# Rearranging two bundles at the start and one R in the middle of a fused convolution and channel mix

## The chip, the cores and the metric

The kernel runs on one core of one Trainium2 chip. The metric is device time in microseconds, from runs of the whole program. A profile is one execution recorded by the hardware profiler; its instructions are read as PE (TensorE matmuls), PEld (TensorE's weight loads), ACT (ScalarE), DVE (VectorE), POOL (GpSimd) and SP (the queue that issues most DMAs).

## The reference

The input x has 8 batches of 4160 rows of 192 values. Two things are computed, one after the other.

- A causal convolution of 7 taps along the rows, with softmax weights that each of 8 heads (24 values wide) has for itself: `y[s] = sum over k of w[h, k] * x[s - 6 + k]`.
- A channel mix of y: with `y_prev` the row before, `xk = y_prev + mu_k * (y - y_prev)` and `xr = y_prev + mu_r * (y - y_prev)`; then `k = relu(xk @ w_k)` (192 to 1024), `v = (k * k) @ w_v` (1024 to 192), `r = sigmoid(xr @ w_r)` (192 to 192), and the output is `r * v`.

## The kernel before

**Pairs, steps, slots, bundles.** Batches go in four pairs; one of a pair lies on partitions 0 to 63 and the other on 64 to 127, a third of the 192 channels at a time. A pair's rows are cut into steps of 512 (the first pair begins and ends with one of 256). A step of 512 has 8 K slots, one of 256 has 4. A K slot (`k_mm`, line 526) makes one PSUM tile of 128 x 2 x 512: 128 of the 1024 hidden values on partitions, for both batches and 512 rows (in a step of 256, twice as many hidden values for half the rows). Four slots are a bundle, and there are 65 bundles, then two last rounds. Their order on every engine is written out by hand: each engine does its instructions in the order in which the program names them (`tc.manual_schedule`, line 937).

**What a bundle holds.** For each of its four slots: `k_mm` on PE, `k_relu` on ACT (PSUM to the SBUF tile k_sb), `k_square` on DVE. Once in it, R (`r`, 12 matmuls; `r_out`, the sigmoid on ACT that empties it) and V (`v_rows`, line 620) for 256 rows of an earlier step: 64 matmuls in two halves, of which `half` 0 ends with a marker that ACT passes only when that half is done. `v_out` (line 643) multiplies both on DVE, which empties V's PSUM tile, and sends the product off through SP. The quads list says which rows each bundle's V takes; it lags the slots.

**The mix.** `diff` (y minus y_prev), `scale` (times mu) and `add_y` (plus y_prev) run on DVE and make xk and xr a bundle or two before they are used. The tables mix_a, mix_b, mix_c and late (lines 713 to 741) say in which bundle and at which of its four places each one stands; `run(table, b)` does what a table holds for bundle b. In the same manner rq and rs hold the R's and the sigmoids of a bundle, and xt its convolution units. rq has one entry for almost every bundle. Of the bundles that bundle_rest runs, only bundle 14 has two, for the second 256 rows of step 6 and the first 256 of step 7; bundle 17 has none.

**The convolution.** x is loaded, as bf16, in groups of rows (lines 88 to 98). For groups 0 to 2 the convolution gives y turned, channels on partitions, straight out of PE. Group 3, in bundle 1, is done as two units: `conv_mm` on PE, `conv_out` on ACT, one cast for the first unit and two for the second, into the tile y with rows on partitions. PE then transposes it (`tr`, line 437: 12 transposes in a first PSUM tile, 3 in a second), and three copies bring it to yT: the first by ACT, the two others by DVE. From group 4 on, a group is four units (`conv_tiles`, 8 matmuls; `conv_tiles_out`, one or two casts on ACT), two in a bundle: group 4 in bundles 2 and 3, group 5 in 4 and 5, later groups in every second bundle. Then `y_write` sends y to DRAM with four DMAs, and `y_read` brings it back with a transposing DMA (lines 416 to 434). For group 4 the write stands at the end of bundle 3, the read in bundle 4, and the first `diff` that needs it in bundle 6.

**PSUM.** All PSUM tiles, those of K, R, V, the transposes and the units, come from one pool of four buffers:

```python
ring = ctx.enter_context(tc.tile_pool(name="ring", bufs=4, space=bass.MemoryType.PSUM))
```

A tile's buffer is free when the last instruction that names it (the relu, sigmoid, product, cast or copy) is done, and the matmul that begins the next tile in that buffer waits for it.

**Who runs the bundles.** bundle_first and bundle_second do bundles 0 and 1, bundle_third does bundle 2, and bundle_rest the others. After bundle 4 a bundle begins with the square of the last slot of the one before, mix_a, and `v_out` of the bundle before; V's second half is the last on PE.

Of the kernel before, what the change touches and what calls it, by code (L numbers as in the profile page):

```python
# [14 lines left out]
def kernel(  # L15
# [11 lines left out]
    nc = tc.nc  # L27
# [33 lines left out]
    for p in range(NPAIR):  # L61
# [5 lines left out]
        for L in sizes:  # L67
            ns = L * NF // STEP
# [8 lines left out]
    bundles, bundle_of = [], {}  # L77
    n = 0
# [86 lines left out]
    n = groups[0][2] * 2 * D  # L165
# [271 lines left out]
    def tr(g, j):  # L437

        p, base, nb, _, _ = groups[g]
        ps = ring.tile([P, 2, 2 * BANK], BF16, tag="k", name="ps_t")  # L440
        todo = range(4 * j, min(nb, 4 * j + 4))
        view = ps[:, :, 0 : 6 * BLK].rearrange("p b (c i t) -> p b c i t", c=3, i=2)
        for i0 in todo[::2]:
            for c in range(3):
                for i in range(i0, min(nb, i0 + 2)):
                    nc.tensor.transpose(
                        out=view[:, (i - 4 * j) // 2, c, i % 2, :],
                        in_=ys[g][:BLK, i, c * P : (c + 1) * P],
                        identity=ident[:BLK, :BLK],
                    )  # L450

        for i in todo[::2]:
            n = min(2, nb - i)
            c0 = YC + base + i * BLK
            (nc.vector.tensor_copy if i else nc.scalar.copy)(
                out=yTs[p][:, :, c0 : c0 + n * BLK].rearrange("p c (n t) -> p c n t", n=n),
                in_=view[:, (i - 4 * j) // 2, :, :n, :],
            )
# [67 lines left out]
    def k_mm(n, cs=range(NC)):  # L526


        s, j = slots[n]
        L = steps[s][2]  # L530
        xk = xks[s]
        if cs[0] == 0 and n not in k_ps:
            k_ps[n] = ring.tile([P, 2, BANK], FP32, tag="k", name="ps_k")
        ps = k_ps[n]
        nf = STEP // L

        for c in cs:
            for f in range(nf):
                fs = slice((j * nf + f) * P, (j * nf + f + 1) * P)
                for i in range(2):  # L540
                    r = slice(i * Q, (i + 1) * Q)
                    nc.tensor.matmul(  # L542
                        out=ps[:, i, f * L : (f + 1) * L],
                        lhsT=wk[r, c, fs],
                        rhs=xk[r, c, :L],
                        start=c == 0 and f == 0,
                        stop=c == NC - 1 and f == nf - 1,
                    )

    def k_relu(n):  # L550
        ps = k_ps.pop(n)
        k_sb = four.tile([P, 2 * STEP], BF16, tag="k_sb", name="k_sb")
        k_sbs[n] = k_sb
        nc.scalar.activation(out=k_sb, in_=ps.rearrange("p a b -> p (a b)"), func=AF.Relu)  # L554

    def k_square(n):
        s, j = slots[n]
        L = steps[s][2]
        k_sb = k_sbs.pop(n)
        if j == 0:  # L560
            k2s[s] = three.tile([P, NF, 2 * STEP], BF16, tag="k2", name="k2")
        nf = STEP // L
        i = k_sb
        o = k2s[s][:, j, :]
        if nf > 1:
            i = k_sb.rearrange("p (b f t) -> p f b t", b=2, f=nf)
            o = k2s[s][:, j * nf : (j + 1) * nf, 0 : 2 * L].rearrange("p f (b t) -> p f b t", b=2)
        nc.vector.tensor_tensor(out=o, in0=i, in1=i, op=ALU.mult)  # L568
# [51 lines left out]
    def v_rows(s, j, half, ks=(0, 1)):  # L620

        if half == 0:
            v_ps[s, j] = ring.tile([P, 2, BANK], FP32, tag="k", name="ps_v")[:, :, 0 : 2 * D]
        for k in ks:
            for f in range(NF):
                for i in range(2):
                    q = slice(i * Q, (i + 1) * Q)
                    bank = (i + half) % 2
                    t = tile_of(s, j, 2 * bank + k)
                    nc.tensor.matmul(  # L630
                        out=v_ps[s, j][:, bank, k * D : (k + 1) * D],
                        lhsT=k2s[s][q, f, t * P : (t + 1) * P],
                        rhs=wv[q, f, :],
                        start=half == 0 and k == 0 and f == 0,
                        stop=half == 1 and k == 1 and f == NF - 1,
                    )
        if half == 0:
            nc.scalar.clobber_nop([nc.scalar.lower_ap(v_ps[s, j])])
# [4 lines left out]
    def v_out(s, j):  # L643
        p, t0, L, _, _ = steps[s]
        o_sb = three.tile([P, 4, D], FP32, tag="o_sb", name="o_sb")
        nc.vector.tensor_tensor(  # L646
            out=o_sb.rearrange("p (b t) d -> p b (t d)", b=2),
            in0=v_ps.pop((s, j)),
            in1=r_sbs.pop((s, j)),
            op=ALU.mult,  # L650
        )
        for st in range(2):
            c = t0 + 2 * j * P
            nc.sync.dma_start(
                out=out[2 * p + st, c : c + 2 * P, :].rearrange("(m p) d -> p m d", p=P),
                in_=o_sb[:, 2 * st : 2 * st + 2, :],
            )
# [24 lines left out]
    early, rq, rs, xt, mix_a, mix_b, mix_c, vq, late = ({} for _ in range(9))  # L682
# [4 lines left out]
    def conv_half(unit, half):  # L687
        if unit is not None:
            conv_mm(*unit, half)
            if half == 1:  # L690
                conv_out(*unit, nc.scalar.copy)

    for g, (p, base, nb, fb, on_pe) in enumerate(groups):
# [12 lines left out]
        if g > 4:  # L706

            b = {5: 1, 6: 2, 7: 7}.get(g)
            b = first_bundle[first_step[p]] + (-15, -11, -7, -3)[(g - 6) % 4] if b is None else b
            table = {5: mix_a, 7: mix_c}.get(g, early)  # L710
# [31 lines left out]
    for s, j, vb in quads:  # L742
        b = vb - (s == LAST)
# [6 lines left out]
        else:  # L750
            vq.setdefault(vb, []).append((s, j))

    def run(table, b):
        for fn, a in table.get(b, ()):
            fn(*a)

    def warm(ps, n):
# [81 lines left out]
    def bundle_second(b, ns):  # L839

        act_, dve_ = nc.scalar.copy, nc.vector.tensor_copy
        g = 2
        k_mm(ns[0])
        k_relu(ns[0])
        k_mm(ns[1])
        tiles = [ring.tile([P, 2, BANK], FP32, tag="k", name="ps_t") for _ in range(2)]
        outs = [tiles[0][:, 0, :], tiles[1][:, 0, :], tiles[0][:, 1, :]]
        conv_t(g, 0, outs[0], range(4))
        to_yT(g, 0, outs[0], 0, 4, dve_)
        k_relu(ns[1])  # L850
        conv_t(g, 1, outs[1], range(4))
        to_yT(g, 1, outs[1], 0, 4, dve_)
        k_mm(ns[2])
        k_relu(ns[2])
        conv_t(g, 2, outs[2], range(4))
        to_yT(g, 2, outs[2], 0, 4, act_)
        k_mm(ns[3])
        k_square(ns[0])
        run(mix_a, b)
        conv_half(xt[b][0], 0)  # L860
        k_relu(ns[3])
        conv_half(xt[b][0], 1)
        k_square(ns[1])
        run(mix_b, b)
        conv_half(xt[b][1], 0)
        conv_half(xt[b][1], 1)
        run(mix_c, b)
        run(late, b)

    def bundle_rest(b, ns):  # L870

        units = xt.get(b, [])
        quad = vq[b][0]
        if b == 4:
            v_out(*vq[b - 1][0])
        for n in bundles[b - 1][2 if b == 3 else 3 :]:
            k_square(n)
        run(mix_a, b)
        if b > 4:
            v_out(*vq[b - 1][0])  # L880
        k_mm(ns[0])
        k_relu(ns[0])
        k_mm(ns[1])
        k_relu(ns[1])
        run(mix_b, b)
        k_square(ns[0])
        k_square(ns[1])
        run(mix_c, b)
        k_mm(ns[2])
        k_relu(ns[2])  # L890
        run(rq, b)
        if units:
            run(rs, b)
        v_rows(*quad, 0)
        if not units:
            run(rs, b)
        k_square(ns[2])
        k_mm(ns[3])
        k_relu(ns[3])
        for u in units:  # L900
            conv_tiles(*u)
            conv_tiles_out(*u)
        v_rows(*quad, 1)
        run(late, b)

    def bundle_third(b, ns):

        quad = vq[b][0]
        for n in bundles[b - 1][2:]:
            k_square(n)  # L910
        run(mix_a, b)
        k_mm(ns[0])
        k_relu(ns[0])
        k_square(ns[0])
        k_mm(ns[1])
        k_relu(ns[1])
        run(rq, b)
        v_rows(*quad, 0)
        run(rs, b)
        tr(3, 0)  # L920
        tr(3, 1)
        k_square(ns[1])
        run(mix_b, b)
        k_mm(ns[2])
        k_relu(ns[2])
        v_rows(*quad, 1, (0,))
        k_mm(ns[3])
        k_relu(ns[3])
        v_rows(*quad, 1, (1,))
        run(mix_c, b)  # L930
        v_out(*quad)
        for u in xt[b]:
            conv_tiles(*u)
            conv_tiles_out(*u)
        run(late, b)

    with tc.manual_schedule():
        prologue()
# [53 lines left out]
```

## Time and profile before

| | |
|---|---|
| median of 4 runs | 415.28 us (415.21 to 415.95) |
| profiled execution | 415.45 us |
| its span, first to last instruction | 413.7 us |
| busy share of the span | PE 98%, DVE 89%, ACT 86%, POOL 16% |
| granted TensorE clock | 1.0 throughout |
| bundle 2, bundle 3 (start of the first K slot to the next bundle's) | 8.20 us, 6.69 us |
| bundle 4, bundle 5, bundle 6 | 6.40, 6.37, 6.01 us |

Rows of the timeline name, in this order, the start in us from the span's start, the time in us from the first instruction's start to the last one's end, the engine, the line of the program, the operation, what it writes and reads (written tile first), the shape written and read, and the count of instructions merged in that row. In brackets stands how long the engine sat idle before it, and what ended that. An engine's instructions overlap somewhat, so a row can end after the next one starts; on PE the ends are modelled. L542 is K, L599 is R, L630 V, L446 a transpose, L302 a unit of the convolution from group 4 on, L351 one of group 3; L554 is the relu, L610 the sigmoid, L397 and L319 the casts, L455 the copies to yT; L568 is the square, L480 diff, L516 scale, L522 add_y, L646 the product; on SP, L424 is y_write, L432 y_read, L654 an output.

### The profile page before, as it was taken

What the parts mean: (1) busy time and instruction counts of PE and PEld (TensorE: products, weight loads), DVE (VectorE), ACT (ScalarE), POOL (GpSimd) and SP (SyncE); (2) the same over time, 40 slices, a digit from 0 to 9 for tenths busy, and PEclk for the clock granted to TensorE, in tenths of its full rate; (3) what the DMA queues carried; (4) which work ended last, traced back from release to release, by engine and by line L of the source; (5) the groups of instructions that cost most, each with busy time, mean ns of one, the idle gap of its engine ahead of it and who ended that gap; (6) DMA issues with size and microseconds to landing.
All of it is one profiled execution on the core that took longest, in us unless ns stands there. A gap on an engine that the chain in (4) does not pass through costs nothing.

```text
span 413.7 us, 16805 instructions
## 1 busy us (share of the span) xinstructions
PE 404.7 (98%) x7349; PEld 302.3 (73%) x7350; DVE 369.2 (89%) x672; ACT 354.4 (86%) x428; POOL 65.5 (16%) x102
## 2 busy tenths in 40 slices
PE   7999999999999999999999999999999999999996
PEld 5567767767777777777777777777777777777795
DVE  5989799999899998989899999989989898999973
ACT  6999978889888888998888899888899888787781
POOL 8760023012040200204040020303000000000000
PEclk9999999999999999999999999999999999999999
DMA  9999989969779895997769698896973926411223
GB/s 146 178 190 203 190 206 188 246 140 189 161 129 215 156 204 138 179 230 113 195 119 233 164 172 194 103 235 118 205 164 90 194 80 160 122 61 59 79 79 115
DMA packets 137657, 65.58 MB, mean 159 GB/s; under 512 B 87388, under 2 KB 137584, under 8 KB 137584
## 3 DMA queue, kind: packets, MB, share of 16 engines
q1 hardware_dynamic: 95840, 48.42, 45.1%
q0 software_dynamic: 40944, 15.53, 33.1%
q8 instruction: 57, 0.93, 0.9%
q10 hardware_dynamic: 800, 0.57, 0.4%
q14 instruction: 16, 0.13, 0.1%
HBM read 31.62 MB, written 37.09 MB: 166 GB/s over the span
## 4 chain that ended last, share of the span: by engine, by line
PE 85%; DMA 4%; ACT 3%; DVE 3%; SPq 2%; issue 1%; POOL 0%; ACTq 0%; POOLq 0%
PE ps_v L630 37%; PE ps_k L542 36%; PE ps_r L599 7%; PE ps_c L302 3%; DMA y_dram<-y 2%; ACT k_sb L554 2%; DMA xb<-in_x_dram 1%; PE ps_v L582 1%; SPq L432 1%; ACT y L319 1%; SPq L424 1%; DVE k L568 1%; DMA out_dram<-o_sb 1%; DVE xk L522 0%; DVE o_sb L646 0%
## 5 line engine op out<-in xcount | busy, mean ns | idle before, releaser
L554 ACT ACTIVATE k_sb<-ps_k 128x1024 bf16<-128x1024 f32 x260 | 253.0, 1037 | 35.7 <-PE ps_k L542 34.2
L568 DVE TENSOR_TENSOR k<-k_sb 128x1024 bf16<-128x1024 bf16 x260 | 172.5, 685 | 29.3 <-ACT k_sb L554 28.9
L542 PE MATMUL ps_k<-xk,wk 64*128 64x512 bf16 (+1 forms) x1632 | 191.0, 367 | 1.1 <-DVE xk L522 0.6
L630 PE MATMUL ps_v<-wv,k 64*128 64x192 bf16 x4032 | 188.3, 243 | 0.1
L630 PEld LDWEIGHTS <-k 64*128 64x128 bf16 x4032 | 168.0, 94 | 13.5 <-issue 4.0
L542 PEld LDWEIGHTS <-wk 64*128 64x128 bf16 x1632 | 80.5, 94 | 59.6 <-issue 1.6
L136 POOL DMA_DIRECT2D xb<-in_x_dram x62 | 45.3, 738 | 176.2 <-issue 81.6
L646 DVE TENSOR_TENSOR o_sb<-ps_v,r_sb 128x768 f32<-128x768 f32 x64 | 60.9, 952 | 2.6 <-issue 2.4
L610 ACT ACTIVATE r_sb<-ps_r 128x768 bf16<-128x768 f32 x65 | 53.2, 821 | 11.1 <-PE ps_v L630 10.4
L319 ACT CAST y<-ps_c 128x960 bf16<-128x960 f32 (+5 forms) x84 | 50.7, 685 | 0.0
L599 PEld LDWEIGHTS <-xr 64*128 64x128 bf16 x780 | 34.5, 94 | 15.9 <-issue 1.9
L599 PE MATMUL ps_r<-wr,xr 64*128 64x192 bf16 x780 | 43.0, 243 | 1.2 <-DVE o_sb L646 1.2
L516 DVE TENSOR_SCALAR xr<-d,mu 128x512 bf16<-128x512 bf16 (+1 forms) x102 | 34.7, 346 | 0.0
L480 DVE TENSOR_TENSOR d<-yT 128x1536 bf16<-128x1536 bf16 (+3 forms) x37 | 31.7, 856 | 2.3 <-ACT yT L381 1.4
L522 DVE TENSOR_TENSOR xr<-xr,yT 128x1536 bf16<-128x1536 bf16 (+1 forms) x33 | 31.0, 939 | 1.1
L516 DVE TENSOR_SCALAR xk<-d,mu 128x512 bf16<-128x512 bf16 (+1 forms) x98 | 31.5, 350 | 0.1
L522 DVE TENSOR_TENSOR xk<-xk,yT 128x1536 bf16<-128x1536 bf16 (+2 forms) x34 | 30.5, 900 | 0.1
L302 PEld LDWEIGHTS <-toe 64*64 64x64 bf16 x448 | 9.5, 106 | 11.4 <-issue 10.6
L302 PE MATMUL ps_c<-xb,toe 64*64 64x240 bf16 (+1 forms) x448 | 16.4, 264 | 0.0
L464 POOL COPY y_tail<-yT 128x195 bf16<-128x195 bf16 x4 | 3.0, 762 | 65.4 <-DMA yT<-y_dram 65.3
L111 POOL MEMSET xb<- 32x384 bf16 x3 | 1.3, 423 | 40.5 <-DVE xb L109 40.5
L371 PEld LDWEIGHTS <-xb 128*32 128x32 bf16 (+3 forms) x264 | 5.4, 120 | 2.4 <-ACT xb L230 1.0
(59 smaller groups left out, 65.5 us busy)
## 6 DMA issues: line engine op xcount, KB each, us to landing
out_dram<-o_sb SPq DMA_DIRECT2D x128, 192.0 KB
xb<-in_x_dram POOLq DMA_DIRECT2D x40, 240.0 KB, 8.5
y_dram<-y SPq DMA_DIRECT2D x44, 210.0 KB
y_dram<-y SPq DMA_DIRECT2D x12, 168.0 KB
xb<-in_x_dram POOLq DMA_DIRECT2D x10, 192.0 KB, 6.0
xb<-in_x_dram POOLq DMA_DIRECT2D x6, 216.0 KB, 7.0
xb<-in_x_dram POOLq DMA_DIRECT2D x6, 144.0 KB, 6.1
wk<-in_moe_w_k_dram POOLq DMA_DIRECT2D x4, 96.0 KB, 5.3
```

The source lines that it names most:

```text
L136: nc.gpsimd.dma_start(out=xb[q0 : q0 + rows, lo:hi, s, :], in_=bass.AP(tensor=x.tensor, offset=x.offset + (b * S + t0 + lo * step) * D, ap ...
L302: nc.tensor.matmul(out=banks[j * Q : (j + 1) * Q, i, :, :, k * G : (k + 1) * G], lhsT=toe[q, h, q], rhs=xbs[g][q, j * m : (j + 1) * m, :, ...
L319: nc.scalar.copy(out=bass.AP(tensor=y.tensor, offset=y.offset + d, ap=[y.ap[0], [m * 2 * D, 2], [2 * D, m], [Q, 2], [1, b - a]],), in_=bas ...
L516: nc.vector.tensor_scalar(out=t[:, c, :L], in0=diffs[s][:, c, :L], scalar1=mu[:, i, c : c + 1], scalar2=None, op0=ALU.mult)
L522: nc.vector.tensor_tensor(out=o, in0=o, in1=y_of(s, sl, 0), op=ALU.add)
L542: nc.tensor.matmul(out=ps[:, i, f * L : (f + 1) * L], lhsT=wk[r, c, fs], rhs=xk[r, c, :L], start=c == 0 and f == 0, stop=c == NC - 1 and f ...
L554: nc.scalar.activation(out=k_sb, in_=ps.rearrange("p a b -> p (a b)"), func=AF.Relu)
L568: nc.vector.tensor_tensor(out=o, in0=i, in1=i, op=ALU.mult)
L599: nc.tensor.matmul(out=ps[:, i, k * D : (k + 1) * D], lhsT=xr[q, c, ts], rhs=wr[q, c, :], start=c == 0, stop=c == NC - 1,)
L610: nc.scalar.activation(out=r_sbs[s, j], in_=r_ps.pop((s, j))[:, :, 0 : 2 * D], func=AF.Sigmoid)
L630: nc.tensor.matmul(out=v_ps[s, j][:, bank, k * D : (k + 1) * D], lhsT=k2s[s][q, f, t * P : (t + 1) * P], rhs=wv[q, f, :], start=half == 0 ...
L646: nc.vector.tensor_tensor(out=o_sb.rearrange("p (b t) d -> p b (t d)", b=2), in0=v_ps.pop((s, j)), in1=r_sbs.pop((s, j)), op=ALU.mult,)
```

## The change

Four edits.

1. The first of `tr`'s three copies goes to DVE too, so that DVE makes all three.
2. In bundle 1, group 3's second unit keeps its matmuls, and its two casts move to bundle 2, behind R, its sigmoid and V's first half.
3. Bundle 2 no longer holds the transposes and group 4's units 0 and 1. The sigmoid is named ahead of V's first half; mix_b, mix_c and late come together behind the second slot's square; the third slot's square is the last step, behind `v_out`. Bundle 3, which has a branch of its own at its head, does two slots first, then the transposes with their copies, the square of bundle 2's last slot, group 4's units 0 and 1, and mix_a; the rest is as in other bundles, with units 2 and 3 behind the fourth slot.
4. `run` can take a part of a table's entries. In bundle_rest a second R, where there is one, and its sigmoid go behind the fourth slot and its relu, between V's halves. Only bundle 14 has one.

```diff
@@ tr
-            (nc.vector.tensor_copy if i else nc.scalar.copy)(
+            nc.vector.tensor_copy(
@@ run
-    def run(table, b):
-        for fn, a in table.get(b, ()):
+    def run(table, b, part=slice(None)):
+        for fn, a in table.get(b, [])[part]:
             fn(*a)
@@ bundle_second
         run(mix_b, b)
-        conv_half(xt[b][1], 0)
-        conv_half(xt[b][1], 1)
+        conv_mm(*xt[b][1], 0)
+        conv_mm(*xt[b][1], 1)
         run(mix_c, b)
@@ bundle_rest
-        if b == 4:
-            v_out(*vq[b - 1][0])
-        for n in bundles[b - 1][2 if b == 3 else 3 :]:
-            k_square(n)
-        run(mix_a, b)
-        if b > 4:
-            v_out(*vq[b - 1][0])
-        k_mm(ns[0])
-        k_relu(ns[0])
-        k_mm(ns[1])
-        k_relu(ns[1])
+        if b == 3:
+            for n in range(2):
+                k_mm(ns[n])
+                k_relu(ns[n])
+            tr(3, 0)
+            tr(3, 1)
+            k_square(bundles[b - 1][3])
+            for u in xt[b - 1]:
+                conv_tiles(*u)
+                conv_tiles_out(*u)
+            run(mix_a, b)
+        else:
+            if b == 4:
+                v_out(*vq[b - 1][0])
+            k_square(bundles[b - 1][3])
+            run(mix_a, b)
+            if b > 4:
+                v_out(*vq[b - 1][0])
+            for n in range(2):
+                k_mm(ns[n])
+                k_relu(ns[n])
         run(mix_b, b)
         k_square(ns[0])
         k_square(ns[1])
         run(mix_c, b)
         k_mm(ns[2])
         k_relu(ns[2])
-        run(rq, b)
+        run(rq, b, slice(0, 1))
         if units:
             run(rs, b)
         v_rows(*quad, 0)
         if not units:
-            run(rs, b)
+            run(rs, b, slice(0, 1))
         k_square(ns[2])
         k_mm(ns[3])
         k_relu(ns[3])
+        run(rq, b, slice(1, None))
+        if not units:
+            run(rs, b, slice(1, None))
         for u in units:
@@ bundle_third
         k_mm(ns[1])
         k_relu(ns[1])
         run(rq, b)
+        run(rs, b)
         v_rows(*quad, 0)
-        run(rs, b)
-        tr(3, 0)
-        tr(3, 1)
+        conv_out(*xt[b - 1][1], nc.scalar.copy)
         k_square(ns[1])
         run(mix_b, b)
+        run(mix_c, b)
+        run(late, b)
         k_mm(ns[2])
         k_relu(ns[2])
         v_rows(*quad, 1, (0,))
         k_mm(ns[3])
         k_relu(ns[3])
         v_rows(*quad, 1, (1,))
-        run(mix_c, b)
         v_out(*quad)
-        for u in xt[b]:
-            conv_tiles(*u)
-            conv_tiles_out(*u)
-        run(late, b)
+        k_square(ns[2])
```

## The prediction

> **What bounds the kernel now.** I read the page's head first, then the PE's own timeline for the stretches in which it stands still, then ACT, DVE and SP in those stretches. Bundle b is four K slots; bundle 2 starts at 20.56 us, bundle 3 at 28.76, bundle 4 at 35.45, bundle 7 at 54.23, bundle 15 at 103.80.
>
> ```profile
> span 413.7 us, 16805 instructions
> PE 404.7 (98%) x7349; PEld 302.3 (73%) x7350; DVE 369.2 (89%) x672; ACT 354.4 (86%) x428; POOL 65.5 (16%) x102
> ```
>
> TensorE is busy for 98% of the span, so an edit pays only where it removes a PE wait, and only if no later wait takes the gain back. After the start I find three stretches with waits. The first is bundles 2 and 3:
>
> ```profile
> 20.56 1.47 PE L542 MATMUL ps_k<-xk,wk 64*128 64x512 bf16 x12
> 21.86 0.68 PE L599 MATMUL ps_r<-wr,xr 64*128 64x192 bf16 x12
> 22.61 1.56 PE L630 MATMUL ps_v<-wv,k 64*128 64x192 bf16 x32
> 24.10 0.96 PE L446 MATMUL ps_t<-ident,y 120*128 120x120 bf16 x15
> 25.16 0.82 PE L542 MATMUL ps_k<-xk,wk 64*128 64x512 bf16 x6
> 28.76 2.33 PE L542 MATMUL ps_k<-xk,wk 64*128 64x512 bf16 x18 [0.27 <-DVE xk L522]
> 35.45 0.81 PE L542 MATMUL ps_k<-xk,wk 64*128 64x512 bf16 x6
> ...
> 20.68 1.88 ACT L397 CAST y<-ps_c 120x960 bf16<-120x960 f32 x3
> 24.98 0.77 ACT L455 COPY yT<-ps_t 128x720 bf16<-128x720 bf16 x1
> 25.79 0.78 DVE L455 COPY yT<-ps_t 128x720 bf16<-128x720 bf16 x2 [1.58 <-ACT yT L455]
> ```
>
> See that V at 22.61 starts as the last cast ends (22.56), that the K slot at 25.16 starts as the sigmoid ends (24.28 + 0.83), and that DVE stands 1.58 us until ACT's copy of the transposes is done, which makes xk late for 28.76. The PSUM ring has four buffers, and these waits fit one rule: a new tile takes the buffer released longest ago in program order.
>
> The second stretch is bundles 6 and 7, the third bundle 15:
>
> ```profile
> 36.52 3.05 SPq L424 DMA_DIRECT2D y_dram<-y  x4
> 43.39 4.85 SPq L432 DMA_TRANSPOSE yT<-y_dram  x1
> 50.22 0.96 DVE L480 TENSOR_TENSOR d<-yT 128x1536 bf16<-128x1536 bf16 x1 [0.84 <-DMA yT<-y_dram]
> 54.23 2.12 PE L542 MATMUL ps_k<-xk,wk 64*128 64x512 bf16 x18
> 56.83 0.67 PE L599 MATMUL ps_r<-wr,xr 64*128 64x192 bf16 x12 [0.48 <-DVE o_sb L646]
> ...
> 99.53 1.15 PE L599 MATMUL ps_r<-wr,xr 64*128 64x192 bf16 x24
> 102.13 1.51 ACT L610 ACTIVATE r_sb<-ps_r 128x768 bf16<-128x768 f32 x2 [0.74 <-PE ps_v L630]
> 103.52 4.01 ACT L554 ACTIVATE k_sb<-ps_k 128x1024 bf16<-128x1024 f32 x4
> 104.59 0.69 DVE L568 TENSOR_TENSOR k<-k_sb 128x1024 bf16<-128x1024 bf16 x1 [1.26 <-ACT k_sb L554]
> 105.66 0.95 DVE L646 TENSOR_TENSOR o_sb<-ps_v,r_sb 128x768 f32<-128x768 f32 x1
> 106.66 0.67 PE L599 MATMUL ps_r<-wr,xr 64*128 64x192 bf16 x12 [0.71 <-DVE o_sb L646]
> ```
>
> At 50.22 DVE waits for group 4's y, which goes out at 36.52 and comes back transposed; from there DVE runs without a pause to the product at 55.82, and the R at 56.83 waits for that. In bundle 14 two sigmoids stand in a row, so the relu of slot 4 starts only at 103.52, its square at 104.59, the product behind it at 105.66, and R of bundle 15 waits for the buffer.
>
> **Part 1: bundle 14's second R.** It is the only bundle run by bundle_rest with two R's. They take 99.53 to 100.52, 0.50 each; moving one costs PE nothing (same 24 matmuls). First half of V then starts at 100.03 and ends its issue at 101.35, the last matmul some 0.2 later; the sigmoid of the first R follows (it waits behind the marker of V's first half) at about 101.65 and lets ACT go on after 0.71, at 102.36. Slot 4 issues from 101.35; a relu starts some 0.9 after its slot's first matmul (35.45 to 36.35), so it is ready at 102.25. Relu 102.36 to 103.4, square to 104.1, the two scales in between 0.38, product 104.5 to 105.45. R of bundle 15 is then free to start when its three slots are issued, at 103.80 + 1.95 = 105.75, in place of 106.66: **0.9 us**. The second sigmoid, now behind the relu (103.3 to 104.1), gives its buffer to the third slot at 105.1, and ACT is free before the first relu of bundle 15 is ready (104.7). Queued behind the second sigmoid are only those relus; cover 0.6. Next in line in bundle 15 are V (buffer of a relu ending 105.7) and the second convolution unit (sigmoid, ends 108.24, wanted near 108.6): no wait. No DMA moves here.
>
> **Part 2: bundles 2 and 3.** Removed: ACT's transpose copy (0.77). Added: one DVE copy of the same 128x720 (0.53, the longer of DVE's two). Moved: two casts of group 3's second unit behind sigmoid and V's first half; the transposes and units 0 and 1 of group 4 behind two slots of bundle 3; DVE's product and a square forward.
> - V's first half takes the buffer of slot 1 in place of the cast's. That relu starts when the first cast ends (21.52) and takes 1.05: V at 22.62, as before. Nothing gained.
> - Slot 3: buffer of slot 2 (relu ends near 23.5), behind V at 23.94. The wait of 25.16 is gone. Slots and V's second half follow: 0.65 + 0.65 + 0.65 + 0.66, so bundle 3 could start at 26.55.
> - xk for it: DVE does two squares (to 24.6), two scales and the add (0.96), without the 1.58 pause: ready at 26.1. No wait; cover 0.45.
> - Bundle 3: two slots to 27.85, transposes 0.9 to 28.75 (the second tile wants bundle 2's product, ready at 28.2). Unit 0 at 28.75; unit 1 wants the second relu, 28.34 to 29.40: a **wait of 0.4**. The third slot wants the first transpose tile, whose two DVE copies run 28.82 to 29.80: a **wait of 0.1**, at 29.85.
> - Then slot 0.65, R 0.49, V from 30.99; from V's start to bundle 4 the row of before has 31.41 to 35.45 with 0.1 of it lost, so 3.94: bundle 4 at 34.93, **0.5 us** early. Queued behind the casts on ACT is one sigmoid and one relu, with 8.3 us of bundle for 7.9 of work.
>
> The price of the DVE copy decides here. The trace has 0.53 on DVE and 0.77 on ACT for one shape. [...]
>
> **What of the 0.5 survives.** Bundle 7 hangs on group 4's y. The last cast before the write ended at 36.50; by the same steps it ends at 35.98 (relu of slot 4 from 33.16, casts behind it), 0.52 early. SP's order doesn't change: bundle 2's output (two DMAs, now some 1.4 earlier than 29.59, among the loads, with nothing waiting for them), write, bundle 3's output, read; so the outputs push nothing. On POOL's queue nothing is moved: group 6's tile and loads stay ahead of bundle 2. But the write now meets the tail of the input loads. [...] The DMA view has 238 packets of SP's queue from 34 to 35 us beside 205 of the loads, and 243 from 38 to 39 beside 45: nearly no loss, 0.5 kept. I take **0.4**, ends 0 and 0.5. PE's own 0.5 is capped by it: bundle 7's R comes 0.4 earlier, and after it no row shows PE waiting for a transfer.
>
> **Sum.** 0.9 + 0.4 = 1.3. The profiled run took 415.45 with a span of 413.7; span 412.4, run 414.15. The median of the runs is 0.17 below the profiled one: **414.0 us**, 0.3% faster. A measurement of this kernel tells some 0.2%, 0.83 us, from no change.
>
> **Rivals.**
> - Only part 1 pays, 0.18: the write meets the loads, or the copies are slow, and y lands at its old time. For it: the loads' queue holds 120% of an engine set's time from 36 to 37. 415.28 - 0.9 = 414.4, on the edge of what can be told.
> - More is gained, 0.10: y lands early enough that bundles 6 and 7 lose their waits too (0.25 and 0.65 against a seamless start), with part 2's 0.5: 415.28 - 0.9 - 0.5 - 0.9 = 413.0. Against it: the write can't start before ACT's casts.
> - Part 1 doesn't do what it says, 0.08: R of bundle 15 waits for another buffer. Only 0.4 is left: 414.9.
> - Slower, 0.14: bundle 3 now holds four convolution units' casts on ACT, 3.5 us beside 4.4 us of relus and sigmoid, in a bundle of 8.3; if the ring makes PE and ACT wait for each other there, group 4's write is late, and each us on it is a us at 50.22. It turns the sum at casts ending 0.9 later than before, at 37.4, and measurably at 38.2; at 38.9 it gives 416.8. Against it: my steps leave 0.5 the other way.
>
> **Numbers.** The forecast has 0.50, its own range 413.5 to 414.5. Faster: nearly all of it, half of the first rival and the second, 0.67; same 0.19; slower 0.14. Range 413.2 to 415.1: it leaves out the slower rival and half of the deeper gain.
>
> **What would show it.** V of bundle 2 still near 22.6; bundle 3 near 26.6, bundle 4 near 34.9; no wait of DVE on ACT at L455; y's write near 36.0, DVE's wait for yT ending near 49.8; R of bundle 7 near 56.4; in bundle 15 R straight after K, 105.75 less 0.4. Wrong would be a longer wait for unit 1 or the third slot of bundle 3, a y that lands no earlier, or a new wait of R.

## The result, and the profile after

The changed kernel takes 414.18 us (median of 31 runs), the kernel before 415.39 us over its runs beside them: a ratio of 0.9972 (95% interval 0.9966 to 0.9977), 1.2 us faster (1.0 to 1.4). The forecast was 414.0, 1.3 us under the median of before. Two later series of the same kernel gave 0.9979 (0.9971 to 0.9987) and 0.9974 (0.9963 to 0.9985).

The execution profiled with this result is not a typical one. A first input load landed late (ACT waits 1.35 us for x_f, where before it waited 0.32), bundle 2 started at 21.55 us where before it started at 20.56, and PE waited for one more load, that of wv, which took 11.6 us from issue to landing in place of 9.5. From the PE timeline of that execution (start, length in us, engine, line, operation, tiles, shapes, count; in brackets the idle time before the row and its releaser):

```profile
21.55 1.47 PE L542 MATMUL ps_k<-xk,wk 64*128 64x512 bf16 x12
22.85 0.67 PE L599 MATMUL ps_r<-wr,xr 64*128 64x192 bf16 x12
24.57 1.49 PE L630 MATMUL ps_v<-wv,k 64*128 64x192 bf16 x32 [1.04 <-DMA wv<-in_moe_w_v_dram]
```

The first V waits for its weights. That execution took 415.79 us, the slowest of the 31. I therefore read the change from a second profile of the same program, after_again (414.21 us, span 412.5). Its head and its PE timeline, for the lines shown of before:

```profile
span 412.5 us, 16801 instructions
PE 403.5 (98%) x7349; PEld 300.9 (73%) x7350; DVE 370.3 (90%) x673; ACT 353.7 (86%) x427; POOL 65.3 (16%) x102
...
20.45 1.47 PE L542 MATMUL ps_k<-xk,wk 64*128 64x512 bf16 x12
...
26.43 1.47 PE L542 MATMUL ps_k<-xk,wk 64*128 64x512 bf16 x12
27.84 0.96 PE L446 MATMUL ps_t<-ident,y 120*128 120x120 bf16 x15
28.73 0.40 PE L302 MATMUL ps_c<-xb,toe 64*64 64x240 bf16 x8
29.29 0.40 PE L302 MATMUL ps_c<-xb,toe 64*64 64x240 bf16 x8 [0.16 <-ACT k_sb L554]
29.71 0.82 PE L542 MATMUL ps_k<-xk,wk 64*128 64x512 bf16 x6
...
34.79 2.11 PE L542 MATMUL ps_k<-xk,wk 64*128 64x512 bf16 x18
```

Bundle 3 starts at 26.43, 5.98 us after bundle 2 in place of 8.20. It holds the transposes and two more convolution units, so the gain is read at bundle 4: 34.79 is 14.34 us after bundle 2 in place of 14.89. Two waits remain where the prediction put them. Unit 1 waits for a relu (it starts 0.56 us after unit 0; two units that wait for nothing, at 32.92 us, take 0.54 together), and the third slot comes some 0.15 us late behind it.

The chain through group 4's y, from SP, DVE and PE of the same profile:

```profile
35.86 3.12 SPq L424 DMA_DIRECT2D y_dram<-y  x4
42.68 4.85 SPq L432 DMA_TRANSPOSE yT<-y_dram  x1
...
49.50 0.96 DVE L480 TENSOR_TENSOR d<-yT 128x1536 bf16<-128x1536 bf16 x1 [0.81 <-DMA yT<-y_dram]
...
56.10 0.67 PE L599 MATMUL ps_r<-wr,xr 64*128 64x192 bf16 x12 [0.47 <-DVE o_sb L646]
```

DVE still waits 0.81 us for y, and R of bundle 7 still waits for DVE: PE is ahead here and y decides. Bundles 14 and 15, from PE, ACT and DVE:

```profile
98.79 0.66 PE L599 MATMUL ps_r<-wr,xr 64*128 64x192 bf16 x12
101.25 0.66 PE L599 MATMUL ps_r<-wr,xr 64*128 64x192 bf16 x12
103.07 2.13 PE L542 MATMUL ps_k<-xk,wk 64*128 64x256 bf16 x36
105.03 0.66 PE L599 MATMUL ps_r<-wr,xr 64*128 64x192 bf16 x12
...
101.59 1.02 ACT L554 ACTIVATE k_sb<-ps_k 128x1024 bf16<-128x1024 f32 x1
102.50 0.82 ACT L610 ACTIVATE r_sb<-ps_r 128x768 bf16<-128x768 f32 x1
...
103.71 0.95 DVE L646 TENSOR_TENSOR o_sb<-ps_v,r_sb 128x768 f32<-128x768 f32 x1
```

The second R (101.25) and its sigmoid (102.50) stand behind the fourth slot; the product ends at 104.66, and R of bundle 15 follows its three slots (103.07 + 1.95) with no wait. From R of bundle 7 to R of bundle 15 it was 49.83 us, and now it is 48.93.

### The profile page after: what moved, and what is told of

The parts are those of the page before. It is cut to its first block, busy times and chain, and to the rows that moved or that the text cites. A ratio compares the mean times of both kernels' runs of the same rounds, so it can differ in the third digit from the quotient of the medians.

```text
span 414.1 us, 16801 instructions
## 1 busy us (share of the span) xinstructions
PE 403.5 (97%) x7349; PEld 301.4 (73%) x7350; DVE 371.3 (90%) x673; ACT 353.7 (85%) x427; POOL 65.3 (16%) x102
## 4 chain that ended last, share of the span: by engine, by line
PE 86%; DMA 5%; POOL 3%; DVE 2%; issue 1%; ACT 1%; SPq 0%; DVEq 0%; POOLq 0%; ACTq 0%
PE ps_v L630 38%; PE ps_k L542 36%; PE ps_r L599 7%; PE ps_c L302 3%; DMA wv<-in_moe_w_v_dram 3%; DMA yT<-y_dram 2%; PE ps_v L582 1%; POOL xb L136 1%; DMA y_dram<-y 1%; POOL wk L208 1%; ACT k_sb L554 1%; DVE k L568 0%; ACT y L319 0%; DVE o_sb L646 0%; SPq L424 0%
## 5 line engine op out<-in xcount | busy, mean ns | idle before, releaser
L516 DVE TENSOR_SCALAR xk<-d,mu 128x512 bf16<-128x512 bf16 (+1 forms) x98 | 32.4, 359 | 0.1
L371 PE MATMUL ps_t<-toe,xb 128*32 128x120 bf16 (+3 forms) x264 | 6.2, 263 | 1.2 <-ACT xb L230 1.2
```

Source lines behind the costliest of these rows:

```text
L516: nc.vector.tensor_scalar(out=t[:, c, :L], in0=diffs[s][:, c, :L], scalar1=mu[:, i, c : c + 1], scalar2=None, op0=ALU.mult)
```

## The experiments

Times are ratios to the kernel before on the same chip, with their 95% interval. For the start I use the distance from bundle 2's first K slot in each profile, since the start itself moves by a us from one execution to the next (bundle 2 at 20.45 us in after_again, at 21.55 in after, where x_f landed late). A wait for a load ahead of bundle 2 is therefore in none of these figures (us):

| kernel | order of bundles 1 to 3 | bundle 4 | y's write issued | y's read issued | R of bundle 7 | read to that R |
|---|---|---|---|---|---|---|
| before | old | 14.88 | 15.95 | 22.82 | 36.26 | 13.44 |
| only_mid | old | 14.88 | 15.95 | 22.39 | 35.80 | 13.41 |
| only_mid_again | old | 15.01 | 16.08 | 22.75 | 36.27 | 13.52 |
| mid_dve | old, copies on DVE | 14.93 | 15.94 | 22.33 | 35.84 | 13.51 |
| after (its V held 1.0 us by wv) | new | 15.30 | 16.37 | 22.78 | 36.12 | 13.34 |
| after_again | new | 14.34 | 15.41 | 22.23 | 35.65 | 13.42 |
| after_third | new | 14.63 | 15.70 | 22.28 | 35.67 | 13.39 |
| only_start | new | 14.80 | 15.87 | 22.19 | 35.75 | 13.56 |
| act_copy | new, a copy on ACT | 15.48 | 16.60 | 22.88 | 36.37 | 13.49 |
| out_behind_new | new | 14.67 | 15.74 | 21.90 | 35.45 | 13.55 |
| out_behind_old (its V held 0.5 us by wv) | old | 15.68 | 16.76 | 23.29 | 36.63 | 13.34 |
| late6_new | new | 14.34 | 15.40 | 21.72 | 35.25 | 13.53 |
| late6_old | old | 14.88 | 15.95 | 22.54 | 36.35 | 13.82 |

The last column is the firm one: wherever the read is issued, R of bundle 7 comes 13.3 to 13.6 us later (13.8 in late6_old). What doesn't move the read does not move bundle 7.

**The change again, and its two parts apart.** after_again is the changed kernel. only_mid is the kernel before with the fourth edit:

```diff
-        run(rq, b)
+        run(rq, b, slice(0, 1))
...
+        run(rq, b, slice(1, None))
+        if not units:
+            run(rs, b, slice(1, None))
```

only_start is the changed kernel with that edit taken back.

> The changed kernel once more, for a second profile: the profiled one began 1.0 us late (bundle 2 at 21.55 in place of 20.56), and its first V waited 1.0 us for the weights wv. If that was this execution's own loads, the stretch from bundle 2 to bundle 4 takes about 14.4 us in place of 15.3, V starts near 2.05 us after bundle 2, and the span is near 412.4. If the new order itself brings the wait for wv, V again starts 3 us after bundle 2. Time: 1.2 us under the kernel before.

> The kernel before with the fourth edit alone: bundle 14's second R and its sigmoid behind the fourth slot. My theory: R of bundle 15 starts as its three K slots end, 0.9 us are gained, 414.5 against 415.4, ratio 0.9978. Rival that the middle pays nothing: ratio 1.000 and R of bundle 15 still behind the product. Rival that only the middle pays: 1.2 us, all of the change.

> The change without its fourth edit, so bundles 1 to 3 and the copies alone. My theory: 0.4 us gained (ratio 0.9990), all that group 4's y allows; bundle 4 some 0.5 us early, R of bundle 7 some 0.4 early, R of bundle 15 still 0.7 us idle. Rival that y lands at its old time or that wv holds V of bundle 2: 0.0, ratio 1.000. Rival that nothing after takes it back: 0.9 or more, ratio 0.998.

Measured: after_again 0.9979 (0.9971 to 0.9987), bundle 2 to 4 in 14.34 us, first V 2.04 us after bundle 2; so the long wait for wv was that execution's. only_mid 0.9984 (0.9977 to 0.9990), 0.7 us, and its profile has the 0.9 us between R of bundle 7 and of bundle 15 (48.94). The fourth edit does what the prediction says, and the rival that it pays nothing falls. The rival that it alone pays does not fall: 1.2 us lies outside its interval, but beside it on the same chip the whole change gained 0.9, and the medians of the two, 414.67 and 414.55, are 0.1 apart, less than their scatter can tell. only_start 0.9994 (0.9982 to 1.0005), which does not tell 0.4 us from nothing; it does shut out the rival of 0.9 or more. In its profile R of bundle 15 keeps its wait.

**One copy back on ScalarE.**

```diff
-            nc.vector.tensor_copy(
+            (nc.vector.tensor_copy if i else nc.scalar.copy)(
```

> The changed kernel with the first of the three copies of the transposes back on ScalarE. My theory: it stands behind the second slot's relu of bundle 3, takes 0.77 us there, VectorE's copies wait for it, the third slot of bundle 3 starts some 0.7 us later and the casts of group 4 too; the 0.4 us of the start are lost and 0.3 more: 414.8, 0.6 us under the kernel before. Rival (the price of a copy is the same on either engine, or hidden): no difference from the change, 414.2.

Measured: 0.9980 (0.9973 to 0.9988), the same as the change beside it, so by the clock the rival won. By the profile the third slot waits for the copy, as worked out. ACT, DVE and PE of act_copy:

```profile
30.33 0.77 ACT L455 COPY yT<-ps_t 128x720 bf16<-128x720 bf16 x1
...
31.13 0.78 DVE L455 COPY yT<-ps_t 128x720 bf16<-128x720 bf16 x2 [1.27 <-ACT yT L455]
...
31.72 0.82 PE L542 MATMUL ps_k<-xk,wk 64*128 64x512 bf16 x6 [0.82 <-DVE yT L455]
```

The third slot waits 0.82 us, bundle 4 comes 1.1 later than in after_again, R of bundle 7 0.7 later. Not all of that is the copy's: 0.35 of the 1.1 are lost already in bundle 2, where V waits for a square on DVE, as it does in only_start, which has no copy on ACT. Part of the 0.7 comes back further on. I set the R's of all bundles against each other, for all profiles with the loads in place. Those of the last series, on another chip, run 0.5 us longer from bundle 15 to the end, spread over all of it and whatever the order; apart from that there is one place after bundle 15 where they differ: bundle 25. ACT, DVE and PE of after_again there, then the same of only_mid:

```profile
161.55 0.81 ACT L610 ACTIVATE r_sb<-ps_r 128x768 bf16<-128x768 f32 x1 [0.52 <-PE ps_v L630]
163.91 0.51 DVE L516 TENSOR_SCALAR xk<-d,mu 128x512 bf16<-128x512 bf16 x1
164.34 0.94 DVE L646 TENSOR_TENSOR o_sb<-ps_v,r_sb 128x768 f32<-128x768 f32 x1
162.96 2.11 PE L542 MATMUL ps_k<-xk,wk 64*128 64x512 bf16 x18
165.34 0.67 PE L599 MATMUL ps_r<-wr,xr 64*128 64x192 bf16 x12 [0.27 <-DVE o_sb L646]
```

```profile
161.37 0.81 ACT L610 ACTIVATE r_sb<-ps_r 128x768 bf16<-128x768 f32 x1 [0.24 <-PE ps_v L630]
163.73 0.35 DVE L516 TENSOR_SCALAR xk<-d,mu 128x512 bf16<-128x512 bf16 x1
164.00 0.95 DVE L646 TENSOR_TENSOR o_sb<-ps_v,r_sb 128x768 f32<-128x768 f32 x1
163.05 2.11 PE L542 MATMUL ps_k<-xk,wk 64*128 64x512 bf16 x18
165.00 0.67 PE L599 MATMUL ps_r<-wr,xr 64*128 64x192 bf16 x12
```

Bundle 24's sigmoid starts 0.52 us after ACT's previous instruction in the one and 0.24 in the other. The relu, the square and a scale behind it come later, that scale takes 0.51 in place of 0.35, the product ends late, and R of bundle 25 starts 2.38 us after its bundle in place of 1.95. The late sigmoid is in all seven profiles with the new order and the copies on DVE (after, after_again, after_third, only_start, out_behind_new, and late6_new and mid6_new below) and in none of before, only_mid, only_mid_again, mid_dve, out_behind_old, late6_old and act_copy. So it belongs to the program, not to chance: the new order pays 0.44 us here, over a hundred us behind bundle 3, and act_copy doesn't. These 0.44 of its 0.7 are what act_copy gets back.

The traces say more of where it comes from. The DMA view has a queue, q14, of kind "instruction", whose packets carry 8,192 bytes each once the kernel runs. These are its rows (packets, MB, share of the 16 DMA engines) for 161 to 163 us of after_again and for 158.8 to 160 us of only_mid:

```profile
q14 instruction: 1, 0.01, 1.7%
```

```profile
q14 instruction: 1, 0.01, 2.9%
```

In all fourteen profiles this packet starts when ACT is at its 320th to 323rd instruction (waits counted), while DVE's place then varies from its 335th to its 344th. What differs is where bundle 24's sigmoid stands in ACT's program:

| profiles | ACT's instructions, waits counted | sigmoid, after the wait in front of it ends | the packet's start, against the sigmoid's |
|---|---|---|---|
| the seven above | 792 | 0.35 to 0.37 us | 0.65 to 0.92 us later |
| act_copy, mid_dve | 794 | 0.07 us | 1.1 us earlier |
| the other five | 795 | 0.07 to 0.09 us | 2.1 to 2.2 us earlier |

The sigmoid is late just where it stands at that place of ACT's program at which this packet starts, and act_copy, whose copy and the wait for it move it on by two instructions, is free of it. That points to the packet. No run moves the sigmoid's place and nothing else, and no trace says that the packet brings ACT's program.

**The copies on DVE alone, in the old order** (mid_dve: only_mid with the first diff line of the change, all three copies on DVE).

> The kernel before with the fourth edit and all three copies of the transposes on VectorE, bundles 1 to 3 in the old order. Theory: VectorE's 1.58 us wait for ScalarE's copy becomes some 0.8 (it waits for the transposes alone), xk of bundle 3 comes 0.3 earlier, bundle 3 starts 0.3 earlier relative to bundle 2 (7.9 us in place of 8.2), and of that 0.1 reaches bundle 7: no difference from only_mid in time. [...]

Measured: 0.9976 (0.9965 to 0.9987) on another chip, not told from only_mid's 0.9984. DVE and PE of its bundle 2:

```profile
25.10 1.22 DVE L455 COPY yT<-ps_t 128x720 bf16<-128x720 bf16 x3 [0.84 <-PE ps_t L446]
...
20.61 1.47 PE L542 MATMUL ps_k<-xk,wk 64*128 64x512 bf16 x12
28.56 0.82 PE L542 MATMUL ps_k<-xk,wk 64*128 64x512 bf16 x6
29.61 1.47 PE L542 MATMUL ps_k<-xk,wk 64*128 64x512 bf16 x12 [0.22 <-DVE o_sb L646]
```

The wait of 1.58 is 0.84, three copies take 1.22 together, bundle 3 starts 7.95 us after bundle 2 in place of 8.19: all as expected. The second slot then waits for the product, and bundle 4 has none of it (14.93). The row's 0.53 for a long copy on DVE holds: in the profile of the result the two long ones take 0.52 and 0.53, the short one 0.34.

**The loads out of y's way.** Group 6's loads are issued in bundle 6 (late6_new on the changed kernel, late6_old on only_mid), or in the middle of bundle 5 (mid6_new), in place of bundle 2:

```diff
-            b = {5: 1, 6: 2, 7: 7}.get(g)
+            b = {5: 1, 6: 6, 7: 7}.get(g)
```

mid6_new has `6: 5` there, and issues the loads behind the second slot's square.

> The changed kernel with group 6's loads issued in bundle 6 in place of bundle 2, so that no load moves while group 4's y is written. Theory (the 0.5 us of the start is lost where the write meets the loads' tail): the write to DRAM takes less than the 6.8 us from issue to the read's issue, some 6.0, the read is issued near 41.9, and R of bundle 7 comes 0.8 earlier relative to bundle 2; 413.4 if group 6's data is there when bundle 7's convolution wants it, near 59. Rival (the chain depends on SP and the write alone): still 6.8, no gain. Against both: bundle 7's convolution waits for group 6's data, up to 2 us, which shows as a wait of PE on that transfer.

> The kernel before with the fourth edit and group 6's loads in bundle 6: the old order of bundles 1 to 3 with the loads out of the way. Theory: it too gets its read earlier, but the new order now keeps its whole 0.5 us over it, where with the loads in bundle 2 the two were 0.1 apart at the read's issue (42.69 and 42.80). So 0.5 us slower than late6_new. Rival: 0.1 to 0.2 slower, as with the loads in the way.

> The changed kernel with group 6's loads issued in bundle 5, behind its second slot's square, near 44.5 us. Theory: as late6_new for the write, the read issued near 41.9, and group 6's data is there 3 us earlier, so bundle 7's convolution doesn't wait; but the loads now meet the transposing read, which can take 1 us longer. 413.4 to 414.2.

Measured: 1.0109 (1.0074 to 1.0143), 1.0133 (1.0106 to 1.0159) and 1.0116 (1.0065 to 1.0166): all slower by some 5 us. The expectation of late6_new allowed for a wait of up to 2 us; 5 us were in none. (mid6_new's ratio rests on three runs.) PE and SP of late6_new show how it begins:

```profile
62.13 1.01 PE L302 MATMUL ps_c<-xb,toe 64*64 64x240 bf16 x14 [2.50 <-DMA xb<-in_x_dram]
...
60.42 8.55 SPq L432 DMA_TRANSPOSE yT<-y_dram  x1
```

Bundle 7's convolution waits 2.5 us for group 6, and group 5's read, issued at 56.09 before, now goes at 60.42 and takes SP 8.55 us among the loads in place of 3.33. From R of bundle 7 to that of bundle 8 it is 11.26 us in place of 6.38; the granted clock from 54 to 70 us is 0.89. The rest of the 5 us is not traced to its causes.

Only the part ahead of that can be read. From the write's issue to the read's it takes 6.31 us in late6_new and 6.58 in late6_old. With loads and output both in place it is 6.28 to 6.87 over nine profiles of the table. So what the loads cost the write does not stand out of the scatter. The 6.0 that I expected was too low: most of this time is not due to the loads. R of bundle 7 comes 1.10 us earlier in late6_new than in late6_old, and the runs are 0.3 us apart by their medians, with a scatter of some us. mid6_new's profile, with a granted clock of 0.988, is not read for these times.

**The output behind the read.** Bundle 4's product still goes to SBUF first, but its two DMAs are issued behind group 4's read, so none is issued between the write and the read (out_behind_new on the changed kernel, out_behind_old on only_mid); beside them the changed kernel and only_mid once more.

```diff
-                v_out(*vq[b - 1][0])
+                v_out(*vq[b - 1][0], send=False)
...
         run(mix_c, b)
+        if b == 4:
+            v_send(*vq[b - 1][0])
```

> The changed kernel with one more edit: the two output DMAs that bundle 4 issues between group 4's write and its read (384 KB) are issued behind the read. Theory (bundle 7 hangs on the write's landing, and the output shares SP's queue and the engines with it): the read is issued 0.5 to 1.3 us earlier, some 21.3 us after bundle 2 in place of 22.2; bundle 7's waits vanish as far as PE's own pace allows, 0.8 at most; 413.7, 0.7 under the change. Rival (landing is set by something else than the shared transfer): read as before, 414.4. Against both: the write of the product comes later, but only the end of the kernel waits for outputs.

> The same edit on the kernel before with the fourth edit, so with bundles 1 to 3 in the old order. Theory: with y out of the way PE's own 0.5 us of the new order come through, so this is 0.5 slower than out_behind_new: read some 21.8 us after bundle 2, 414.2. Rival (the new order's 0.5 is lost elsewhere too): no difference from out_behind_new.

> The changed kernel beside the two above, on one chip. Theory: read 22.2 us after bundle 2, V of bundle 2 some 2.05 after it (3.0 only where this execution's loads are late), 414.4.

> The kernel before with the fourth edit alone, beside the other three. Theory: read 22.5 us after bundle 2, 0.1 to 0.3 us slower than the change; the new order and the old differ less here than where the output goes behind the read. Rival: the start pays its 0.4 in full here, 0.4 slower.

Measured: 0.9975 (0.9965 to 0.9985), 0.9987 (0.9978 to 0.9996), 0.9974 and 0.9984 (0.9976 to 0.9993). SP and PE of out_behind_new:

```profile
35.98 3.05 SPq L424 DMA_DIRECT2D y_dram<-y  x4
42.14 3.53 SPq L432 DMA_TRANSPOSE yT<-y_dram  x1
...
55.69 0.67 PE L599 MATMUL ps_r<-wr,xr 64*128 64x192 bf16 x12 [0.22 <-DVE o_sb L648]
```

From write to read it is 6.16 us, 0.4 to 0.7 shorter than in after_third and after_again, but only 0.16 shorter than in only_start; out_behind_old has 6.53, and only_mid, with the output in place, 6.44. The read comes 21.90 us after bundle 2, where 21.3 was expected, and R of bundle 7 35.45, 0.2 earlier than in after_third. That the output costs the write anything is not shown, and as a version this does not beat the change. New order against old, on one chip, is 0.10% here (0.9974 to 0.9984) and 0.12% with the output moved (0.9975 to 0.9987), after 0.05% in the first series: 0.1 to 0.5 us. The 0.5 us that were expected of the pair with the output moved are there by the medians (414.70 and 415.15), but the pair beside it is 0.25 apart, and the intervals overlap. In the profiles R of bundle 7 lies 1.18 us apart in this pair, of which 0.2 is wv's, and 1.10 in the pair of late6, against 0.15 and 0.60 with everything in place. The two orders may lie further apart once y's way is free; single profiles, 0.5 apart within one order, do not show it.

## Why the prediction was right, and where it was not

**Part 1, bundle 14's second R: right in every link.** 0.9 us were worked out, and R to R it is 49.83 - 48.93 = 0.90. The nine profiles with the edit and the loads in place have 48.93 to 49.00; before and only_start, without it, have 49.83 and 49.82. The order of first sigmoid, relu, square and product, and the buffer that R waits for, are those of the working.

**Part 2, up to bundle 4: right where nothing else is late.** Bundle 3 was put at 6.0 us after bundle 2 and came, in after_again, at 5.98; bundle 4 was put at 14.4 and came at 14.34; unit 1's wait of 0.4 is 0.3. The row's price of the copy, 0.53, holds: the three copies take 1.22 together. In after_third, only_start and out_behind_new bundle 4 comes at 14.63 to 14.80, and in the profile of the result at 15.30, for two reasons that the working lacked.

**What was missing in part 2: wv and a square.** The working let V of bundle 2 wait for slot 1's buffer alone. Its weights land at nearly the same time (22.26 in the profile of before, V at 22.61), and in three of the five profiles with the new order, the copies on DVE and the loads in place, V starts within 0.05 us of their landing: at 22.62, 22.68 and, where the loads were late, at 24.57. There this load, and not the relu, sets V, which then starts 0.3 to 1.0 us later than the 2.05 us after bundle 2 that it needs otherwise. The old order is not spared it: in out_behind_old V stands 0.61 us until wv is there. In only_start V waits, in its middle, for a square:

```profile
23.90 1.00 PE L630 MATMUL ps_v<-wv,k 64*128 64x192 bf16 x20 [0.17 <-DVE k L568]
```

It lasts 0.35 us longer there. "What is late next" was asked of the buffers, not of the transfers and squares.

**What survives at bundle 7: about right, with a wide scatter.** 0.4 of the 0.5 us were to arrive. The 0.1 between them was my estimate, and no run shows a price that the write pays beside the loads: from its issue to the read's it takes 6.28 to 6.87 us with loads and output there, 6.31 and 6.58 without the loads. R of bundle 7 comes 36.04 us after bundle 2 on average in the first four profiles of the old order in the table (35.80 to 36.27), and 35.69 in after_again, after_third and only_start: 0.35. The profile of the result, whose V waited for wv, has 36.12. With single profiles 0.5 apart in the same order, this does not separate 0.4 from the whole 0.5, nor surely from nothing. That y's read sets this R, the reason given for the cap, is what the table's last column shows.

**After bundle 7: wrong.** "After it no row shows PE waiting for a transfer" was true, but the step from there to a gain that lasts to the end did not hold. At bundle 25 the new order loses 0.44 us. By the profiles the ledger is 0.90 + 0.35 - 0.44 = 0.8 us. The runs gave 1.2, 0.9 and 1.1. The 0.3 us between are within what the series scatter, and within what single profiles of the start do; I can't assign them. So part of the agreement of 1.3 with 1.2 is luck: the gain of part 1 is there, that of part 2 at bundle 7 is about there, and a loss that the forecast lacked, as large as part 2's gain, is hidden by the scatter of the start. From bundle 2 to the end after_again takes 392.02 us and only_mid, on the same chip, 391.75. That edits 1 to 3 shorten the whole is not shown.

**The rivals.** "Only part 1 pays" gave 414.4. By the net account of the start, 0.35 - 0.44, it may well be so, and more likely than its 0.18 said, though for another reason than y's landing. "More is gained" fell: bundle 7 keeps its waits. "Part 1 doesn't do what it says" fell with only_mid. "Slower" fell: y's write, which follows the casts of bundle 3, is issued 0.54 us earlier after bundle 2 in after_again, and not later in after_third and only_start.

## What to carry to other kernels

An edit that takes a wait off the busiest engine is worth what the next event on that path allows, and that event can be a transfer as well as a buffer (here V of bundle 2 waited 1.0 us for wv): list the landing times beside the buffers for each instruction that is to start earlier. Measure a gain as the distance between two events on one engine inside a profile, not by the end of the run: 0.90 us stood out to within 0.07 between two R's, where whole runs of one kernel scatter by 2 us. And follow the distance to the end: a reordering can cost time far behind it, at a place that has no slack (here 0.44 us at bundle 25), and two versions with equal times need not have equal stages.

## What was not expected of the hardware

- The sigmoid in front of bundle 25 starts 0.28 us late in one order of the program and not in another, with the same work in front of it on PE and ACT, and does so in every profile of that order. The order changes only the start of ACT's instruction stream. The number of busy instructions doesn't explain it: mid_dve has 427 on ACT like the changed kernel, and no late sigmoid. Its stream with waits has 794 instructions, though, and the changed kernel's 792, and the late sigmoid stands where a packet of 8,192 bytes of queue q14 starts, 0.65 to 0.92 us behind it. That this packet is the cause is likely by these fourteen traces, and not tested.
- A scale on DVE can take 0.51 us in place of 0.35 beside POOL's issue of loads, and where in the issue it falls counts. In after_again it starts 0.33 us into an issue of 0.72 us and takes 0.51; in only_mid it starts 0.05 us into the same issue and takes 0.35. Of the 37 scales of this shape that touch such an issue in after_again, 27 take 0.33 to 0.39 us and 10 take 0.41 to 0.63. In the profile of the result, too, 37 touch an issue: the 19 that start up to 0.12 us or from 0.49 us into it take 0.33 to 0.35, and of the 18 that start from 0.21 to 0.46 us into it 14 take 0.38 to 0.71. Of the 148 that touch none, 146 take 0.33 to 0.35.
- The write of 840 KB to DRAM takes 6.2 to 6.9 us from its first issue to the read that waits for it. It scatters by 0.6 us with the same transfers beside it, and taking away the loads (6.31 and 6.58) or the output (6.16 and 6.53) makes no difference that stands out of that.
